# The head of an attention and feed-forward kernel: maxima on VectorE, half of the q sums on TensorE, and a new order of the instructions

## The chip, the cores and the metric

The kernel runs on one core of a Trainium2 chip. The metric is the time of one execution on the device in microseconds; of several runs the median is given. A profile is one such execution, recorded instruction by instruction.

## The reference, cut to what matters

```python
# q, k, v: 8 batches, 8 heads, 576 rows, 64 columns
q_s = exp(q - max over the 64 columns);  q_s /= sum over the 64 columns + 1e-9
k_s = exp(k - max over the 576 rows);    k_s /= sum over the 576 rows + 1e-9
kv  = einsum('bhsd,bhse->bhde', k_s, v)
x   = einsum('bhsd,bhde->bhse', q_s, kv)      # as 4608 tokens x 512
h   = x @ w_in                                # 512 -> 2048
out = (max(h, 0) + log1p(exp(-abs(h)))) @ w_out   # 2048 -> 512
```

Any shift that is the same over a normalised axis gives the same softmax up to the 1e-9, which the kernel uses below. The two weights come as 64-bit floats.

## The kernel before, in words

The 4608 tokens are cut into nine tiles of 512. The first three tiles go through the feed-forward part plainly; the other six go in pairs, as products of 2 x 2 blocks with seven instead of eight products. Each 512-column product of 32-bit numbers is made of three products of rounded high and low parts; only the first two of the sixteen weight blocks are used unsplit for tile 0.

Nothing schedules the kernel at run time: a long table `ORDER` names every step of the program in turn, and each engine executes its own steps strictly in that order, waiting by semaphores for the other engines. This document is about the head of the table, up to the first product with `w_out`. Its steps are:

- `b0 b1` fetch the q values of tile 0 in two halves, each as two transfers (`q_fetch`). `n` fetches keys and values of two heads at once (`kv_load`): 512 KB of main part on SyncE's DMA queue and a 64 KB tail on ScalarE's. The four pairs of heads of batch 0 are called pairs 0 to 3 here; in the order's rows the first two lie in tiles `kvt`, the others in `x_...`.
- `k0.h.i` is step i of pair h (`kv_unit`): 0 `top`, 1 `turn`, 2 `across`, 3 `spread`, 4 `shift`, 5 `power` (exp on ScalarE), 6 `product` (sums and k-times-v products on TensorE), 7 `scale` (a reciprocal on VectorE), 8 `keep` (two scaled copies on ScalarE). Before, `top` does nothing for batch 0; `turn` transposes the whole of k on TensorE into one PSUM bank, `across` takes the maximum along that bank on VectorE in three instructions (L500, L501, L504), `spread` sends it back to all partitions (L507), `shift` subtracts it (L511).
- `q0.i` are the steps of q's softmax on tile 0 (`q_unit`): a maximum by halves on VectorE (L580), four small copies on ScalarE that bring the neighbour's maximum (L567), their maximum (L591), subtraction (L594, one half on VectorE and one on GpSimd), exp (L597), sum by halves on VectorE (L600), one product with the matrix `pair` for each half (L607), which adds the sum of the other 32 rows, reciprocal (L625, L626), multiplication (L629).
- `x0.h.i` (`x_first`) transposes the normalised q, multiplies it by the kept k-times-v and copies the result; `B` is the first `w_in` block on it (L712), `U1` the second, `A0` the first softplus (L733 on ScalarE), `O0` the first product with `w_out` (L762).
- `T`, `M`, `S`, `J`, `P`, `Q` turn the 64-bit weights into 32-bit high and low parts on ScalarE, VectorE and GpSimd.
- `w` is a number of products of the identity with itself (L1163), whose result nobody reads.

ScalarE works through weight conversion and attention in one row, so a step of the one can wait behind a step of the other. The functions that the change touches:

Of the kernel before, what the change touches and what calls it, by code (L numbers as in the profile page):

```python
# [19 lines left out]
P = 128  # L20
# [32 lines left out]
    w0.20 b0 b1 q0.0 n k0.0.1 n q0.1 n n q0.2 q0.3 q0.4.1 l0 q0.5 l1 k0.0.2 k0.1.1 l2 k0.1.2 k0.0.3 k0.2.1 k0.0.4  # L53
    k0.0.5 q0.6 k0.1.3 k0.2.2 w5.5 k0.2.3 k0.1.4 k0.2.4 k0.1.5 l3 q0.7 k0.3.1 k0.3.2 k0.0.6 k0.0.7 T0 M0.1 T1 k0.1.6
    q0.8 k0.3.3 q0.12 w1.6 q0.13 k0.2.5 k0.2.6 k0.3.4 k0.3.5 k0.3.6 n M1.1 k0.0.8 q0.9 q0.10 w2.3 k0.1.7 w3.2 k0.2.7
    k0.1.8 k0.2.8 x0.0.0 w4.2 T2 x0.1.0 x0.1.1 x0.0.2 k0.3.7 k0.3.8 q0.11.1 x0.2.0 x0.3.0 x0.1.2 l4 J0 x0.3.1 x0.2.2
    k1.0.0 B0 B1 M2.1 n J1 T3 M3 x0.3.2 k1.0.1 k1.0.2 J2 S3.1 T4 M4.1 B2 B3 l5.6.7.8.9 L1 k1.0.3 k1.0.4 U0 k1.1.0
    k1.0.5 J4 U1 A0 k1.0.6 x0.2.3 k1.0.7 x0.2.4 O0 J3 P2 Q2 x0.0.3 x0.0.4 x0.1.3 T5 x0.3.3 x0.1.4 k1.1.1 x0.3.4 k1.1.2
    P3 Q3 A1 M5 k1.0.8 U2 T8 k1.1.3 k1.1.4 U3 P4 A2 q1.0 S5.1 T9 Q4 A3 G2 M6.1 O1 J5 G3 U4 k1.1.5 P5 O2 T6 M8.1 Q5.1
    k1.1.6 M7.1 T7 k1.2.0 k1.2.1 J6 J8 P6 k1.1.7 k1.2.2 q1.1 U5 A4 Q6 A5 J7 O3 U6 G4 G5 P7 M10 Q7 k1.1.8 O4 M9 q1.2  # L60
    T12 k1.3.0 U7 S9 q1.3 P8 A6 Q8 J9 T11 T10 A7 G6 q1.4 k1.3.1 O5 D4 P9 k1.2.3 G7 S10 M14.1 k1.2.4 q1.6 k1.3.2 O6
    M11.1 Q9 k1.2.5 U8 J11 A8 J10 P10 Q10 T14 U9 q1.8 A9 G8 M12.1 k1.2.6 k1.3.3 O7 P11 M13.1 Q11 J12 k1.3.4 G9 T13 P12
    q1.5 J13 q1.7 U10 Q12 J14 O8 U11 k1.3.5 A10 O9 k1.3.6 k1.2.7 U12 P13 A11 T15 Q13 q1.9 G10 q1.11 q1.10 P14 O10
    x1.0.0 A12 G11 U13 Q14 M15.1 k1.2.8 J15 x1.2.0 k1.3.7 P15 k1.3.8 Q15.1 U14 x1.1.0 A13 G12 D3 x1.1.3 O11 x1.3.0 U15
    G13 x1.0.4 x1.1.4 O12 x1.1.5 A14 x1.0.5 P0 Q0.1 k2.0.0 D6 G14 x1.3.3 D5 x1.2.4 k2.1.0 O13 x1.2.5 x1.3.4 P1 L2
    x1.3.5 D0 A15 Q1.1 G15 O14 k2.0.1 U16 k2.0.2 A16 D15 O15 U17 U18 A17 G16 k2.1.1 q2.1 Y0.1 k2.1.2 O16 G17 Y1.0 Y0.0
    q2.0 U19 k2.0.3 O17 A18 k2.1.3 k2.0.4 D1 G18 k2.1.4 Y0.2 D2 k2.0.5 q2.2 q2.3 Y1.2 D12 k2.1.5 Y2.1 A19 q2.5 O18
    Y1.1 D9 k2.1.6 k2.0.6 G19 D10 k2.0.7 q2.4.1 U20 Y2.0 Y2.2 n O19 U21 Y1.3 Y2.3 A20 Y0.3 D13 k2.0.8 Y2.4 Y2.5 G20
    Y1.4 O20 k2.2.0 U22 Y3.0 k2.1.7 A21 k2.2.1 D7 G21 k2.2.2 q2.6 q2.8 Y0.4 Y0.5 Y2.6 n D8 U23 q2.7 A22 k2.1.8 k2.2.3
    k2.3.0 Y3.2 O21 U24 G22 k2.3.1 k2.2.4 A23 q2.9 Y0.6 k2.3.2 A24 O22 q2.10 k2.3.3 k2.2.5 L3 Y1.5 H1.7.0 q2.11 x2.0.0  # L70
    D11 D14 k2.3.4 Y3.1 Y2.7 H1.7.1 U25 k2.2.6 k2.3.5 Y4.0 k2.2.7 Y2.8 k2.3.6 Y4.1 Y3.3 A25 Y1.6 O23 H1.8.0 U26 Y0.7
    k2.3.7 n A26 U27 Y3.4 x2.1.0 Y3.5 x2.2.0 H1.9.0 H1.8.1 O24 A27 Y3.6 H1.9.1 q3.0 O25 Y3.7 k2.3.8 k2.2.8 Y4.2
    H1.10.0 k3.0.0 n R0.0 Y3.8 H1.11.0 U28 k3.1.0 H1.10.1 x2.1.3 A28 q3.1 Y5.0 Y4.3 q3.12 x2.1.4 O26 Y0.8 Y4.4 k3.0.4
    H1.12.0 U29 q3.2 x2.1.5 U30 q3.3 k3.1.4 Y4.5 x2.0.4 H1.11.1 O27 x2.0.5 H1.12.1 A29 Y1.7 A30 U31 x2.3.0 H1.13.0
    x2.3.3 H1.13.1 k3.0.5 k3.1.5 q3.5 O28 q3.4 Y6.0 x2.3.4 Y7.1 R0.1 Y7.0 O29 x2.2.4 x2.2.5 R0.2 R0.3 q3.7 x2.3.5
    H1.14.0 Y6.1 L4 y0.1 H1.14.1 q3.6 A31 y0.0 R2.0 k3.1.6 Y7.2 k3.0.6 k3.0.7 Y1.8 Y6.2 Y4.6 q3.8 O30 H1.15.0 H1.15.1
    U32 n O31 n q3.13 y0.2 y1.0 A32 Y7.3 F1.0 Y4.7 U33 Y6.3 Y7.4 F1.2 Y6.4 q3.9 H2.0.0 k3.2.0 F1.3 y0.3 k3.3.0 R0.4
    y1.1 k3.2.4 A33 H2.1.0 U34 H2.0.1 F1.1 O32 k3.1.7 k3.2.5 k3.1.8 q4.0 q3.10 H2.1.1 y0.4 Y6.5 k3.0.8 y0.5 O33 k3.3.4
    A34 y1.2 k3.3.5 y2.0 k3.2.6 H2.2.0 Y4.8 q3.11 k3.3.6 H2.2.1 k3.2.7 U35 U36 R0.5 R0.6 y0.6 q4.1 Y7.5 A35 x3.1.0 n
    y0.7 y2.1 y1.3 y1.4 k3.3.7 q4.12 A36 k3.2.8 x3.0.0 y2.2 y1.5 U37 y1.6 n q4.2 q4.4 O34 k3.3.8 A37 H2.3.0 x3.2.0  # L80
    H2.3.1 k4.0.0 H2.4.0 q4.6 y0.8 k4.1.0 q4.3 q4.5 x3.3.0 k4.0.4 x3.1.3 x3.0.6 y1.7 O35 H2.4.1 k4.0.5 U38 O36 x3.1.6
    R0.7 x3.3.3 X0.1.hB11 R0.8 k4.1.4 k4.1.5 Y7.6 U39 A38 q4.8 x3.2.6 H2.5.0 q4.7 x3.3.6 y1.8 y3.1 q4.13 H2.5.1 A39
    X0.0.hB11 k4.0.6 q4.9 R0.9 n Y6.6 Y5.2 k4.1.6 k4.0.7 q4.10 O37 H2.6.0 U40 Y7.7 q4.11 H2.7.0 n H2.6.1 x4.1.0 Y6.7
    A40 x4.0.0 U41 k4.2.0 H2.7.1 R0.10 y4.0 X0.0.lB11 O38 y3.0 y2.3 Y7.8 R0.11 O39 y3.2 Y5.1 H2.8.0 k4.2.4 A41 k4.0.8
    y4.1 U42 Y5.3 k4.3.0 k4.1.7 R0.12 H2.8.1 O40 x4.2.0 k4.2.5 k4.3.4 U43 Y5.4 k4.3.5 y2.4 H2.9.0 k4.1.8 y4.2 A42 y4.3
    H2.10.0 A43 X0.1.lB11 y2.5 Y5.5 H2.9.1 y3.3 y4.4 k4.3.6 Y6.8 k4.2.6 H2.10.1 O41 R0.13 Y5.6 k4.2.7 k4.3.7 y5.0
# [124 lines left out]
def tile_attn_ffn(  # L211
# [1004 lines left out]
```

## Time and profile before

| | |
|---|---|
| median of 3 runs | 810.38 us (808.61 to 810.49) |
| the profiled execution | 809.8 us |
| its span, first instruction to last | 808.0 us |
| TensorE busy | 795.7 us (98%) |
| VectorE, ScalarE, GpSimd busy | 581.9, 499.7, 119.6 us |

The profiled execution lies 1.8 us above its span and 0.6 us under the median. TensorE's ends are modelled, so its busy time counts from one instruction's start to its modelled end; where instructions follow each other without a gap it reads as 100%.

### The profile page before, as it was taken

To read this page: it belongs to the slowest core of one execution; us is meant where nothing else is said; L and a number is where in the kernel's file an instruction comes from. 1 tells how busy PE (TensorE), PEld (TensorE's weight loads), DVE (VectorE), ACT (ScalarE), POOL (GpSimd) and SP (SyncE) were. 2 spreads that over 40 slices of the span, in tenths; PEclk is the share of its full clock that TensorE was granted. 3 is DMA by queue.
4 is the path that set the end of the run, shared out by engine and by line. 5 is a ranking of instruction groups with operands and counts; after the bars stand their busy time and mean duration, and the time that the engine had idled before them with its cause. 6 is when DMAs were issued, how large, how long until landed. Compare 5 with 4: busy or idle time off the path is not lost.

```text
span 808.0 us, 12020 instructions
## 1 busy us (share of the span) xinstructions
PE 795.7 (98%) x4312; PEld 637.7 (79%) x4312; DVE 581.9 (72%) x934; ACT 499.7 (62%) x826; POOL 119.6 (15%) x211
## 2 busy tenths in 40 slices
PE   7999999999999999999999999999999999999997
PEld 6668877887787878878788778887777888888886
DVE  6979764877799878549689898477688943136884
ACT  2999964674577557557768574658466633336651
POOL 1320021101011210001010004240000220400026
PEclk9999999999999999999999999999999999999999
DMA  9996176869788898889789448994483865858655
GB/s 302 360 323 239 30 238 260 307 207 343 256 279 279 290 334 294 292 244 294 233 247 303 151 166 251 299 283 158 141 259 124 262 196 178 266 175 287 193 159 88
DMA packets 118235, 193.73 MB, mean 240 GB/s; under 512 B 8416, under 2 KB 90592, under 8 KB 108960
## 3 DMA queue, kind: packets, MB, share of 16 engines
q1 hardware_dynamic: 114912, 186.67, 70.0%
q0 software_dynamic: 2944, 6.04, 3.6%
q8 instruction: 34, 0.56, 0.3%
q10 hardware_dynamic: 320, 0.26, 0.1%
q14 instruction: 25, 0.20, 0.1%
HBM read 149.95 MB, written 42.99 MB: 239 GB/s over the span
## 4 chain that ended last, share of the span: by engine, by line
PE 94%; DMA 2%; ACT 1%; issue 1%; DVE 1%; POOL 0%; SPq 0%; DVEq 0%
PE po L965 7%; PE po L967 6%; PE po L966 6%; PE po L851 6%; PE po L853 6%; PE po L852 6%; PE po L766 5%; PE ph L724 5%; PE ph L725 5%; PE ph L726 5%; PE po L768 5%; PE po L767 5%; PE ph L851 3%; PE ph L853 3%; PE ph L852 3%; PE ph L965 3%
## 5 line engine op out<-in xcount | busy, mean ns | idle before, releaser
L1010 POOL DMA_DIRECT2D out<-w x92 | 59.4, 653 | 232.0 <-DVE w L1002 230.5
L766 PE MATMUL po<-w,g_hi 128*128 128x512 f32 x164 | 65.6, 400 | 0.0
L724 PE MATMUL ph<-x,w 128*128 128x512 f32 x164 | 65.3, 398 | 0.0
L945 ACT CAST g_hi<-w 128x512 fp32r<-128x512 f32 x74 | 45.8, 621 | 29.8 <-PE po L966 17.2
L768 PE MATMUL po<-w,g_lo 128*128 128x512 f32 x164 | 64.0, 390 | 0.0
L767 PE MATMUL po<-w,g_hi 128*128 128x512 f32 x164 | 64.0, 390 | 0.0
L726 PE MATMUL ph<-x,w 128*128 128x512 f32 x164 | 63.9, 390 | 0.0
L725 PE MATMUL ph<-x,w 128*128 128x512 f32 x164 | 63.9, 390 | 0.0
L948 DVE TENSOR_TENSOR g_lo<-w,g_hi 128x512 fp32r<-128x512 f32 x74 | 50.1, 684 | 11.4 <-ACT g_hi L945 11.1
L742 DVE TENSOR_TENSOR g_lo<-g,g_hi 128x512 fp32r<-128x512 f32 x46 | 32.7, 712 | 32.1 <-ACT g_hi L739 32.1
L733 ACT ACTIVATE g<-ph 128x512 f32<-128x512 f32 x48 | 28.6, 599 | 39.3 <-PE ph L726 39.1
L932 DVE TENSOR_TENSOR w<-w,w 128x512 f32<-128x512 f32 x72 | 47.5, 683 | 5.6 <-ACT w L885 5.6
L479 POOL PARTITION_ALL_REDUCE mx<-mx x20 | 23.0, 1150 | 189.6 <-DVE mx L476 186.4
L874 DVE TENSOR_TENSOR w<-po,w 128x512 f32<-128x512 f32 x24 | 16.3, 684 | 45.6 <-PE po L853 24.7
L945 ACT CAST w<-w 128x512 fp32r<-128x512 f32 x52 | 31.8, 619 | 22.5 <-PE po L966 14.8
L851 PE MATMUL po<-w,x 128*128 128x512 f32 x112 | 44.2, 394 | 0.3 <-DMA x<-sums 0.3
L852 PE MATMUL po<-w,x 128*128 128x512 f32 x112 | 43.6, 389 | 0.0
L853 PE MATMUL po<-w,x 128*128 128x512 f32 x112 | 43.6, 389 | 0.0
L948 DVE TENSOR_TENSOR w<-w,w 128x512 fp32r<-128x512 f32 x52 | 35.3, 684 | 10.9 <-ACT w L945 10.7
L739 ACT CAST g_hi<-g 128x512 fp32r<-128x512 f32 x46 | 28.3, 620 | 21.2 <-PE po L767 14.0
L476 DVE TENSOR_REDUCE mx<-kvt 128x128 f32<-128x640 f32 x28 | 36.7, 1312 | 5.6 <-DMA kvt<-in_kv_tail 4.4
L766 PEld LDWEIGHTS po<-w,g_hi 128*128 128x128 f32 x164 | 30.8, 188 | 10.2 <-issue 1.7
(380 smaller groups left out, 2253.2 us busy)
## 6 DMA issues: line engine op xcount, KB each, us to landing
x<-sums SPq DMA_DIRECT2D x24, 1024.0 KB, 5.6
kvt<-in_kv SPq DMA_DIRECT2D x30, 512.0 KB, 6.8
kept<-w SPq DMA_DIRECT2D x15, 1024.0 KB, 8.8
w<-kept SPq DMA_DIRECT2D x13, 1024.0 KB, 7.1
x<-sums_out SPq DMA_DIRECT2D x44, 256.0 KB, 4.3
w<-kept SPq DMA_DIRECT2D x36, 256.0 KB, 5.4
x<-kept SPq DMA_DIRECT2D x36, 256.0 KB, 4.8
w<-sums_out SPq DMA_DIRECT2D x36, 256.0 KB, 5.3
```

What stands on the lines that cost most here:

```text
L724: nc.tensor.matmul(ph, lhsT=w_hi, rhs=x_hi, start=h == 0, stop=False)
L725: nc.tensor.matmul(ph, lhsT=w_lo, rhs=x_hi, start=False, stop=False)
L726: nc.tensor.matmul(ph, lhsT=w_hi, rhs=x_lo, start=False, stop=h == HP - 1)
L766: nc.tensor.matmul(po, lhsT=g_hi[:, ms], rhs=w_hi, start=j == 0, stop=False)
L767: nc.tensor.matmul(po, lhsT=g_hi[:, ms], rhs=w_lo, start=False, stop=False)
L768: nc.tensor.matmul(po, lhsT=g_lo[:, ms], rhs=w_hi, start=False, stop=j == NJ - 1)
L851: nc.tensor.matmul(ph, lhsT=w_hi, rhs=x_hi, start=c == 0 and i in (0, 4), stop=False, **more)
L852: nc.tensor.matmul(ph, lhsT=w_lo, rhs=x_hi, start=False, stop=False, **more)
L853: nc.tensor.matmul(ph, lhsT=w_hi, rhs=x_lo, start=False, stop=c == 1, **more)
L945: nc.scalar.copy(ring[p, i, s][0], right_of(p, i, s))
L948: engine.tensor_tensor(out=lo, in0=right_of(p, i, s), in1=hi.bitcast(F32), op=ALU.subtract)
L965: nc.tensor.matmul(bank, lhsT=w_hi, rhs=hi, start=begin, stop=False, **more)
```

## The change

- `top` now does work for batch 0: three maxima on VectorE reduce the five chunks of k to one (256, 128 and 128 columns wide). `turn` is then one transpose (L494) instead of ten, and `across` one reduction over 128 columns (L498).
- Tile 0's q gets a function of its own, `q_first`. The neighbour's maximum comes by one product for each half with a new matrix `other_half` (made by one subtraction on VectorE). The sum of a half can be taken on VectorE as before (`total`, L661) or on TensorE, as 32 accumulating products of `pair` with every 32nd column (L664); the new order takes the first half on TensorE and the second on VectorE. Each half has its own reciprocal.
- The two reciprocals of neighbouring pairs are taken by one instruction each (`scale`).
- The eight fills of the padding go from VectorE to GpSimd; GpSimd's first instruction that needs its library (`g`) comes behind them. One of q's two transfers of each half goes onto ScalarE's DMA queue, so q's four transfers stand two on each queue.
- There are fewer idle products of the identity (25 where there were 38), and they stand at other places.
- The rest of `ORDER` is new from end to end. The steps after the head are the same ones but stand in a changed sequence.

```diff
     def top():
+            mx = state["mx"] = sm.tile([P, 2, D], F32, name="mx", bufs=3)
             if not b:
+                two = sm.tile([P, 2, 2, D], F32, name="two")
+                for o, i0, i1 in (
+                    (two, kt[:, 0:2], kt[:, 2:4]), (mx, two[:, 0], two[:, 1]), (mx[0:TAIL], mx[0:TAIL], kt[0:TAIL, NCH]),
+                ):
+                    nc.vector.tensor_tensor(out=o, in0=i0, in1=i1, op=ALU.max)
                 return
...
         def turn():
-            if not b:
-                for c in range(NCH, -1, -1):
-                    rows = P if c < NCH else TAIL
-                    for z in range(2):
...
             nc.tensor.transpose(wide, state["mx"].rearrange("p z d -> p (z d)"), ident)
...
-                nc.sync.dma_start(out=qtiles[t][z * D:(z + 1) * D, 2 * g:2 * g + 2], in_=src[z, g])
+                queue = nc.sync if t or not z else nc.scalar
+                queue.dma_start(out=qtiles[t][z * D:(z + 1) * D, 2 * g:2 * g + 2], in_=src[z, g])
...
+    def q_first():
...
+        def cross(g):
+            nc.tensor.matmul(sums[:, (2 + g) * n:(3 + g) * n], lhsT=other_half, rhs=m[:, g], start=True, stop=True)
...
+        def total(g, on_pe=None):
+            if on_pe is None:
+                nc.vector.tensor_reduce(out=s[:, g], in_=half[g], op=ALU.add, axis=AX.X)
+                return
+            for e in range(32):
+                nc.tensor.matmul(
+                    sums[:, g * n:(g + 1) * n], lhsT=pair, rhs=half[g][:, :, e], start=e == 0, stop=e == 31
+                )
...
-    w0.20 b0 b1 q0.0 n k0.0.1 n q0.1 n n q0.2 q0.3 q0.4.1 l0 q0.5 l1 k0.0.2 k0.1.1 l2 k0.1.2 k0.0.3 k0.2.1 k0.0.4
...
+    w0.9 b0 b1 n n n n g q0.0 l0 q0.2 q0.1 w1.5 w2.2 q0.4 q0.3 w3.5 k0.0.0 q0.5 q0.6 q0.8 k0.0.1 k0.1.0 k0.0.2 w4.4
```

On TensorE's queue the head before had this, from the transposes of pair 2 (`x_178`) to the last spread (`m_266`, pair 3):

```order
L490 MATMUL po_126<-ident,x_178 64x128 x8
L507 MATMUL po_125<-ident,m_220 128x128
L1163 MATMUL ph_128<-ident 128x128 x5
L507 MATMUL po_126<-ident,m_239 128x128
L490 MATMUL ph_128<-ident,x_183 64x64 x2
L490 MATMUL po_127<-ident,x_183 64x128 x8
L522 MATMUL att_93<-one,kvt 64x1 x10
L527 MATMUL po_124<-kvt 64x64 x10
L522 MATMUL att_94<-one,kvt 64x1 x10
L527 MATMUL po_125<-kvt 64x64 x10
L507 MATMUL po_127<-ident,m_266 128x128
```

and the changed kernel has this in that place (`x_154` is pair 2, `x_159` pair 3, `po_128` the bank of pair 3):

```order
L494 MATMUL po_126<-ident,mx 128x128
L501 MATMUL po_125<-ident,m_201 128x128
L494 MATMUL po_127<-ident,mx 128x128
L501 MATMUL po_126<-ident,m_218 128x128
L664 MATMUL ph_130<-qt,pair 128x32 x32
L494 MATMUL po_128<-ident,mx 128x128
L669 MATMUL ph_130<-s,pair 128x32
L501 MATMUL po_127<-ident,m_235 128x128
L501 MATMUL po_128<-ident,m_275 128x128
L516 MATMUL att_93<-one,kvt 64x1 x10
```

The 32 products of the first q half (L664) now stand ahead of the transpose of pair 3's maxima (`po_128<-ident,mx`) and of the spreads of pairs 2 and 3, where the ten transposes of pair 3 stood free of them.

On VectorE's queue the same stretch was, from the shift of pair 2 to the multiplication of q's first half:

```order
L511 TENSOR_TENSOR x_178<-x_178,po_126 128x10x64
L600 TENSOR_REDUCE s<-qt 128x32
L500 TENSOR_REDUCE m_266<-ph_128 128x1
L501 TENSOR_TENSOR po_127<-po_127,m_266 128x1
L504 TENSOR_REDUCE m_266<-po_127 128x1
L535 TENSOR_SCALAR r<-att_93 128x1
L536 RECIPROCAL r<-r 128x1
L600 TENSOR_REDUCE s<-qt 128x32
L511 TENSOR_TENSOR x_183<-x_183,po_127 128x10x64
L625 TENSOR_SCALAR s<-ph_129 128x64
L626 RECIPROCAL s<-s 128x64
L629 TENSOR_TENSOR qt<-qt,s 128x1024
```

and is now, from pair 2's `across` on:

```order
L498 TENSOR_REDUCE m_235<-po_127 128x1
L505 TENSOR_TENSOR kvt<-kvt,po_126 128x10x64
L661 TENSOR_REDUCE s<-qt 128x32
L498 TENSOR_REDUCE m_275<-po_128 128x1
L672 TENSOR_SCALAR s<-ph_130 128x32
L675 RECIPROCAL s<-s 128x32
L672 TENSOR_SCALAR s<-ph_130 128x32
L675 RECIPROCAL s<-s 128x32
L505 TENSOR_TENSOR x_159<-x_159,po_128 128x10x64
L505 TENSOR_TENSOR x_154<-x_154,po_127 128x10x64
L531 TENSOR_SCALAR r_330<-att_93 128x2
L534 RECIPROCAL r_330<-r_330 128x2
```

One of the two long sums (L600, now L661) is gone; pair 3's `across` (`m_275`) is followed by both reciprocals, and the shifts of pairs 3 and 2 have moved behind them.

## Rows read from the trace of the kernel before

**Rows 1.** The page's first part: busy us, share of the span, instructions.

```profile
PE 795.7 (98%) x4312; PEld 637.7 (79%) x4312; DVE 581.9 (72%) x934; ACT 499.7 (62%) x826; POOL 119.6 (15%) x211
```

**Rows 2.** TensorE by stretch: length, busy us (records), granted clock, DMA share, GB/s.

```profile
3.00:5.00 2.00, 2.00 (x9) 1.00 1.03 277
12.00:14.00 2.00, 0.18 (x4) 1.00 1.02 408
14.00:16.00 2.00, 2.00 (x21) 0.53 1.03 412
100.00:700.00 600.00, 597.70 (x3200) 1.00 0.76 247
```

**Rows 3.** Timeline of TensorE at 40 us: start, length, line, operands, count.

```profile
40.93 3.42 PE L762 MATMUL po<-w,g 128*128 128x512 f32 x7
```

**Rows 4.** Timeline of ScalarE from 20 to 41 us; in brackets the idle time before.

```profile
23.68 0.73 ACT L517 ACTIVATE x<-x 128x640 f32<-128x640 f32 x1
25.03 0.74 ACT L517 ACTIVATE x<-x 128x640 f32<-128x640 f32 x1 [0.62 <-DVE x L511]
...
27.76 1.28 ACT L542 ACTIVATE kvs<-po,r 64x64 f32<-64x64 f32 x4 [0.42 <-DVE r L535]
...
30.61 0.58 ACT L691 COPY x<-po 128x512 f32<-128x512 f32 x1 [0.36 <-PE po L650]
...
40.27 0.60 ACT L733 ACTIVATE g<-ph 128x512 f32<-128x512 f32 x1
```

**Rows 5.** Timeline of VectorE from 5 to 13 us.

```profile
6.39 1.22 DVE L580 TENSOR_REDUCE m<-qt 128x32 f32<-128x1024 f32 x1 [2.86 <-DMA qt<-in_q]
...
9.86 1.22 DVE L580 TENSOR_REDUCE m<-qt 128x32 f32<-128x1024 f32 x1 [1.59 <-DMA qt<-in_q]
...
12.14 0.22 DVE L591 TENSOR_TENSOR m<-m,other 128x64 f32<-128x64 f32 x1 [0.40 <-ACT other L567]
12.40 1.22 DVE L594 TENSOR_TENSOR qt<-qt,m 128x1024 f32<-128x1024 f32 x1
```

**Rows 6.** Timeline of SyncE's DMA issues up to 17 us.

```profile
0.75 2.81 SPq L560 DMA_DIRECT2D qt<-in_q  x4
3.60 1.07 SPq L454 DMA_DIRECT2D kvt<-in_kv  x2
```

**Rows 7.** Timeline of all engines up to 42 us: TensorE and its weight loads.

```profile
2.98 6.77 PE L1163 MATMUL ph<-ident 128*128 128x128 f32 x40 [2.98 <-DVE ident L260]
...
10.86 1.09 PE L490 MATMUL po<-ident,kvt 128*64 128x128 f32 x16 [0.84 <-DMA kvt<-in_kv]
...
20.83 0.70 PE L522 MATMUL att<-one,kvt 128*64 128x1 f32 x20
...
24.87 0.30 PEld L607 LDWEIGHTS ph<-s,pair 128*128 128x128 f32 x2
24.98 0.31 PE L607 MATMUL ph<-s,pair 128*128 128x32 f32 x2
```

**Rows 8.** The same timeline: VectorE.

```profile
16.89 0.81 DVE L511 TENSOR_TENSOR kvt<-kvt,po 128x640 f32<-128x640 f32 x1
...
20.55 1.21 DVE L600 TENSOR_REDUCE s<-qt 128x32 f32<-128x1024 f32 x1
...
25.32 0.23 DVE L625 TENSOR_SCALAR s<-ph 128x64 f32<-128x64 f32 x1 [0.33 <-PE ph L607]
...
25.58 0.55 DVE L626 RECIPROCAL s<-s 128x64 f32<-128x64 f32 x1
```

**Rows 9.** Timelines of 33 to 37 us: VectorE.

```profile
35.03 0.29 DVE L504 TENSOR_REDUCE m<-att 128x1 f32<-128x128 f32 x1 [0.42 <-PE att L495]
```

**Rows 10.** Timeline of GpSimd up to 24 us.

```profile
9.49 0.18 POOL L1065 TENSOR_TENSOR first<-first 128x1 f32<-128x1 f32 x1 [8.65 <-issue]
12.45 2.95 POOL L594 TENSOR_TENSOR qt<-qt,m 128x1024 f32<-128x1024 f32 x1 [2.77 <-DMA kvt<-in_kv]
22.37 0.20 POOL L450 MEMSET kvt<- 64x128 f32 x1 [6.97 <-issue]
```

More of the change, by code (lines that the diff above doesn't have):

```diff
@@ L58 @@
[L58 to L62, printed above, removed]
@@ L241, in tile_attn_ffn @@
     pair = const.tile([P, P], F32, name="pair")
+    other_half = const.tile([P, P], F32, name="other_half")
     one = const.tile([P, 1], F32, name="one")
@@ L267, in make_tables @@
             )
+        nc.vector.tensor_tensor(out=other_half, in0=pair, in1=ident, op=ALU.subtract)
         nc.vector.memset(one, 1.0)
@@ L604, in swap @@
         def swap(g):
-            if not t:
-                nc.tensor.matmul(sums[:, 0:2 * n][:, g], lhsT=pair, rhs=s[:, g], start=True, stop=True)
-                return
             if not other:
@@ L633, in q_unit, with spread, top, join @@
             lambda: total(0), lambda: total(1), invert, lambda *e: divide(0, *e), lambda *e: divide(1, *e),
-        ] + ([cross, swap_all] if t else [lambda g=g: swap(slice(g * n, (g + 1) * n)) for g in range(2)])
+            cross, swap_all,
+        ]
+    def q_first():
+        n = TOK // 16
+        half = [qtiles[0][:, 2 * g:2 * g + 2].rearrange("p h (i r) -> p (h i) r", r=32) for g in range(2)]
+        m, s = (sm.tile([P, 2, n], F32, name=name) for name in ("m", "s"))
+        def spread(a, g):
+            return a[:, g].unsqueeze(2).broadcast_to([P, n, 32])
+        def top(g):
+            nc.vector.tensor_reduce(out=m[:, g], in_=half[g], op=ALU.max, axis=AX.X)
+        def cross(g):
+            nc.tensor.matmul(sums[:, (2 + g) * n:(3 + g) * n], lhsT=other_half, rhs=m[:, g], start=True, stop=True)
+        def join(g):
+            nc.vector.tensor_tensor(out=m[:, g], in0=m[:, g], in1=sums[:, (2 + g) * n:(3 + g) * n], op=ALU.max)
+        def shift(g, engine=nc.vector):
+            engine.tensor_tensor(out=half[g], in0=half[g], in1=spread(m, g), op=ALU.subtract)
+        def power(g):
+            nc.scalar.activation(half[g], half[g], AF.Exp)
+        def total(g, on_pe=None):
+            if on_pe is None:
+                nc.vector.tensor_reduce(out=s[:, g], in_=half[g], op=ALU.add, axis=AX.X)
+                return
+            for e in range(32):
+                nc.tensor.matmul(
+                    sums[:, g * n:(g + 1) * n], lhsT=pair, rhs=half[g][:, :, e], start=e == 0, stop=e == 31
+                )
+        def swap(g):
+            nc.tensor.matmul(sums[:, g * n:(g + 1) * n], lhsT=pair, rhs=s[:, g], start=True, stop=True)
+        def invert(g):
+            nc.vector.tensor_scalar(
+                out=s[:, g], in0=sums[:, g * n:(g + 1) * n], scalar1=EPS, scalar2=None, op0=ALU.add
+            )
+            nc.vector.reciprocal(s[:, g], s[:, g])
+        def divide(g, engine=nc.vector):
+            engine.tensor_tensor(out=half[g], in0=half[g], in1=spread(s, g), op=ALU.mult)
+        return [
+            lambda *e, g=g, f=f: f(g, *e)
+            for f in (top, cross, join, shift, power, total, swap, invert, divide) for g in range(2)
+        ]
     def x_part(t, h):
@@ L1165, in do @@
                 q_fetch(0, at)
+            elif kind == "g":
+                nc.gpsimd.tensor_tensor(out=first, in0=first, in1=first, op=ALU.add)
             elif kind == "n":
-                place = dict(engine=nc.vector, queue=nc.scalar) if ahead[0] < HP else {}
+                place = dict(queue=nc.scalar) if ahead[0] < HP else {}
                 if 2 <= ahead[0] < HP:
```

329 lines of the change are left out of this document (163 added, 166 removed).

## The prediction

> **What bounds the kernel now.** I read the page's first part, then TensorE by stretches, then the timelines of the first 41 us engine by engine. The profile's page says that TensorE is busy for 795.7 us, 98% of the span [rows 1]. The stretches say where it is not: from 100 to 700 us it lacks 2.3 us in 600 [rows 2], so behind the head the kernel is a dense row of products whose number the change leaves alone. What can move the time by much is therefore the moment at which this row begins, and whether the new order tears holes into it. I take as its beginning the first product with `w_out`, at 40.93 us [rows 3]; it waits for the first softplus, which ScalarE starts at 40.27 us [rows 4].
>
> ScalarE is the engine to follow backwards from there. Its timeline is almost closed from the third pair's exp at 23.68 us to the softplus at 40.27 us; the idle times in it are 0.62, 0.42 and 0.36 us [rows 4]. So between these two points lie 16.59 us, of which 15.2 us are work: two exps, eight kept copies, three copies of x, seven conversions of weights, the exp of the next batch's pair and a table load. By the code the new order has the very same instructions between its third k exp and its softplus, in another sequence. Hence one question decides: when does the third k exp start? If it starts 1.4 us later than now, at 25.1 us, and ScalarE then never waits, the softplus stands where it stood.
>
> Ahead of it VectorE is the engine to follow. Its first maximum waits until 6.39 us and its second until 9.86 us for q; the small copies on ScalarE cost it 0.40 us more, and it begins to subtract at 12.40 us [rows 5].
>
> **When pair 0 is there.** The new VectorE order needs the keys of pair 0 before it can join and subtract q's second maximum. Today TensorE takes them up at 10.86 us [rows 7]. SyncE issues q's four transfers in 2.81 us and the keys from 3.60 us on [rows 6]; with two of the four on ScalarE's queue the keys are issued 1.4 us earlier. If the issue sets the landing they land at 9.5 us. But the transfer engines are already full from 3 to 5 us (share 1.03, [rows 2]), and the same q bytes plus the tails still stand ahead. Then they land at 10.8 us. I take 10.2, between the two, since neither end has a row that excludes it. The Trainium skill, page DMA: Bandwidth & Descriptors, section Issuing engines are not separate DMA queues, says that transfers issued from several engines run on the same DMA engines and interleave. By that rule the split gains nothing here, the keys land at 10.8 us, and the sum below would be 810.2 us instead of 809.6; by the issue times alone it would be 808.9.
>
> **VectorE from pair 0 to pair 1's spread.** A full half of 1024 columns takes 1.22 us [rows 5], 640 columns 0.81 us [rows 8]; the slope gives about 0.40 us for 256 and 0.27 us for 128 columns, so a new `top` costs 1.0 us with its two inner waits. The transpose ends on VectorE in a reduction of 0.29 us [rows 9]. The row is: top 1.0, join 0.2 (as L591, [rows 5]), subtraction 1.2, top 1.0, across 0.3, top 1.0, across 0.3: 5.0 us, plus 0.1 for TensorE's spread. TensorE comes to the 32 products at 10.2 + 5.1 = 15.3 us. What the edits of this stretch remove (the fills, the copies on ScalarE, the long transposes) is already in this: q is subtracted at 12.4 us, as before, because a `top` of pair 0 stands ahead, and later VectorE has one long sum of 1.21 us [rows 8] less.
>
> **The 32 products.** They are the term that decides, and no row shows such a run. Each is a full 32-bit product, so it leaves two records with a load of 128 weight columns each, as the two records of L607 show: 64 loads. Bounds: the one-column products L522 run 20 records in 0.70 us, 0.035 us each, with half as many weight columns [rows 7]; that gives 64 x 0.035 = 2.2 us. At the other end, between 3 and 5 us nine records of the idle products take 2 us, 0.22 each [rows 2]; that gives 14.2 us. The nearest row has the same matrix and the same 32 columns: the load of L607 starts at 24.87 us and its product at 24.98 us, 0.11 us later, and the second load ends 0.30 us after the first began [rows 7]. I take 0.11 us for each load: 64 x 0.11 = 7.0 us. The products end at 22.3 us.
>
> The Trainium skill's page TensorE: Matmul & The Clock Gate, section LDWEIGHTS, makes a load cost its columns over 1.2 GHz; for 128 columns an estimate of 0.107 us, 6.8 us for the run, as the row has it. The Trainium skill lists on the same page, section Back-to-back issue gap, about 60 cycles for up to 64 moving columns; by that the run would take an estimated 1.6 us, and the time would be that of the first rival.
>
> **From there to the third exp.** Pair 3's transposed maxima stand behind the products on TensorE. Behind them come: the transpose 0.3, the reduction 0.3, two reciprocals with their additions 1.1 (for 64 columns 0.23 and 0.55 us, [rows 8]; for 32 I take 0.19 and 0.36 from the same fixed part), the subtraction 0.8 [rows 8], and a hand-over of 0.1: 2.6 us. The third exp starts at 22.3 + 2.6 = 24.9 us, the softplus at 24.9 + 15.2 = 40.1 us, 0.2 us before today's.
>
> VectorE meanwhile has, after pair 1's across at 15.2 us, only 4.1 us of work that does not need pair 3's transpose (a shift, the last top, an across, a shift, one sum): it stands idle from 19.3 to about 22.6 us. That is where the gain of the rebuilt head goes: 3.3 us of waiting for TensorE.
>
> **What costs nothing, and its cover.** GpSimd's first library instruction ends its wait at 9.49 us today [rows 10]. With eight fills of 0.20 us ahead [rows 10] it ends near 11.1 us; GpSimd's subtraction is asked for at 11.4 us, so it is hidden, and without that cover it would cost 0.3 us. Its exp stands behind pair 0's exp on ScalarE anyway. ScalarE issues two more transfers before its first exp, in time in which it waits for q. The extra subtraction for `other_half` lies in VectorE's wait for q, 2.86 us long [rows 5]. SyncE now fetches the next tile's q ahead of weight blocks 5 to 9; they are needed only after the first `w_out` product. At the very end of the kernel the last steps of each engine stand in the same sequence as before.
>
> **The sum.** 809.8 - 0.2 = 809.6 us against the profiled execution; the median of the runs shown is 0.6 us above that, so I predict 810.0 us.
>
> **The rivals.**
> 1. The products are cheap (2.2 us, the lower bound). They end at 17.5 us, VectorE is not held up, and the third exp follows its own row: 19.3 + 0.3 + 1.1 + 0.8 + 0.1 = 21.6 us, 3.5 us better than 25.1: 806.3 us. For it speaks that 32 columns are little work; against it the gap of 0.11 us at L607.
> 2. TensorE runs the products at half clock. Between 12 and 14 us it is busy for 0.18 us, and from 14 to 16 us the granted clock is 0.53, the lower level of 1.2 GHz for nearly all of it [rows 2]. The head after has 13 idle products fewer, and the new 32 stand just behind such a thin stretch. At 0.22 us a record they end 7.1 us later: 816.9 us, slower. It decides from 2.6 us of extra time on, that is if more than 24 of the 64 records run so. Against it: the 40 records of the idle products at the start take 6.77 us, 0.17 each [rows 7], so a continuous run gets faster on the way. Half of the run at that rate would be 813. The Trainium skill, page TensorE: Matmul & The Clock Gate, Part 1, says the same of an idle array: it falls back to half clock, and activity releases it. How it takes a long run of weight loads no run here shows.
> 3. The new order tears a hole into the dense part. Today's holes are 2.3 us in 600 [rows 2]; a second set and a little more is 2.5 us or over: about 813 us.
> 4. q's two halves really arrive side by side and pair 0 lands before 8 us: 807.6 us or less.
>
> **How the numbers follow.** My forecast, no measurable change, gets 0.55 with a range of its own of 808 to 812 (keys at 9.5 to 10.8 us, a partial clock fall, small holes). Rival 1 gets 0.17, rival 4 0.05, rival 2 in its slow form 0.10, rival 3 0.13. Under 0.3% (2.4 us) a measurement of this kernel tells little from no change. So faster 0.22, same 0.55, slower 0.23. The range reaches to rival 1 below and to rival 3 above and leaves out rival 2's full form and the far end of rival 4: 806.0 to 813.5 us.
>
> **What would show it.** In the profile after: the 32 products as one run of 64 records from about 15 us; its length (7 us, or 2, or 14) tells the first three cases apart. VectorE idle before pair 3's across by about 3 us; the third k exp near 25 us; the softplus near 40 us; TensorE between 100 and 700 us busy for about 597.7 us again. I am wrong if ScalarE waits for something else on its way (kept copies for their reciprocals, x for TensorE), if weight block 0 lands so late that its conversion pushes the exps, or if the dense part has changed.

## The result, and the profile after

The changed kernel takes 821.65 us (median of 4 runs, 819.55 to 822.0), the kernel before beside it 809.5 us (4 runs, 808.4 to 810.49). The ratio is 1.0142, with a 95% interval of 1.0123 to 1.0161: slower by 12 us. The profiled execution took 821.59 us, its span is 819.8 us. The forecast was 810.0 us, with a range of 806.0 to 813.5 us.

The page's first part says that TensorE is busier than before by 9.9 us, with 36 records fewer (columns as in [rows 1]):

```profile
PE 805.6 (98%) x4276; PEld 647.2 (79%) x4276; DVE 586.3 (72%) x929; ACT 509.5 (62%) x830; POOL 121.9 (15%) x219
```

So fewer records take more time. TensorE by stretches (columns as in [rows 2]) says where:

```profile
12.00:14.00 2.00, 0.30 (x3) 1.00 1.01 401
14.00:16.00 2.00, 0.52 (x2) 1.00 1.04 416
16.00:18.00 2.00, 1.92 (x12) 0.71 1.02 406
18.00:22.00 4.00, 4.00 (x21) 0.50 1.04 412
...
34.00:38.00 4.00, 4.00 (x80) 0.50 0.84 205
...
42.00:44.00 2.00, 2.00 (x9) 0.50 1.17 240
44.00:53.00 9.00, 8.39 (x40) 0.99 1.05 302
100.00:700.00 600.00, 598.57 (x3203) 1.00 0.75 244
```

One stretch of the changed kernel, and under it two of the kernel before, in the same columns:

```profile
16.80:44.10 27.30, 27.30 (x244) 0.50 0.62 202
```

```profile
14.13:17.54 3.41, 3.41 (x31) 0.50 1.04 416
17.60:41.00 23.40, 23.20 (x290) 1.00 1.02 366
```

In the changed kernel the granted clock is 0.50, that is 1.2 GHz, from 16.8 to 44.1 us without a break, although TensorE is busy throughout. Before, it was at half for 3.41 us only. The dense part from 100 to 700 us is as it was (598.57 us busy, 597.70 in [rows 2]).

TensorE's timeline (start, length, line, operands, count) shows the run of the 32 products, the x products and the first product with `w_out`:

```profile
16.44 13.37 PE L664 MATMUL ph<-qt,pair 128*128 128x32 f32 x64
...
39.59 3.69 PE L699 MATMUL po<-w,kvs 64*64 64x512 f32 x16
...
52.63 1.62 PE L811 MATMUL po<-w,g 128*128 128x512 f32 x3
```

The last row answers to [rows 3]: the dense row of products begins at 52.63 us instead of 40.93, 11.7 us later. From there to the end of the span it is 767.17 us, before 767.07 us. So the whole loss lies in the head, as the forecast said that it would.

ScalarE's timeline, from the exps of the third and fourth pair to the first softplus (brackets: the idle time before, and what ended it), answers to [rows 4]:

```profile
32.10 1.46 ACT L511 ACTIVATE x<-x 128x640 f32<-128x640 f32 x2 [9.74 <-DVE x L505]
...
34.73 1.34 ACT L545 ACTIVATE kvs<-po,r 64x64 f32<-64x64 f32 x4 [0.16 <-DVE r L534]
...
39.00 1.35 ACT L545 ACTIVATE kvs<-po,r 64x64 f32<-64x64 f32 x4 [1.74 <-DVE r L534]
41.64 1.07 ACT L740 COPY x<-po 128x512 f32<-128x512 f32 x2 [1.29 <-PE po L699]
...
48.11 0.74 ACT L511 ACTIVATE kvt<-kvt 128x640 f32<-128x640 f32 x1 [0.64 <-DMA qt<-in_q]
...
51.25 0.60 ACT L782 ACTIVATE g<-ph 128x512 f32<-128x512 f32 x1
```

The third exp waits 9.74 us, and starts at 32.10 us where 24.9 was forecast. Behind it ScalarE waits for 3.83 us more (0.16, 1.74, 1.29, 0.64), each time for something that TensorE made late, but for the last, which the profile puts down to a transfer.

VectorE's timeline, and under it GpSimd's, show what ended the one long wait and another stall ahead of it:

```profile
11.97 0.43 DVE L483 TENSOR_TENSOR two<-kvt 128x256 f32<-128x256 f32 x1
12.43 2.10 DVE L483 TENSOR_TENSOR mx<-two 128x128 f32<-128x128 f32 x1
...
30.11 0.29 DVE L498 TENSOR_REDUCE m<-po 128x1 f32<-128x128 f32 x1 [10.12 <-PE po L494]
```

```profile
12.48 1.90 POOL L654 TENSOR_TENSOR qt<-qt,m 128x1024 f32<-128x1024 f32 x1
```

VectorE stood for 10.12 us until the transpose of pair 3's maxima, queued behind the run, was done. And a maximum of 128 columns took 2.10 us while GpSimd subtracted; the same one takes 0.29 us for the other pairs.

The instructions of the run by line (durations in ns, least, median, most; first and last start) have two sorts of loads:

```profile
L664 PEld LDWEIGHTS ph<-qt,pair x64: 187/333/338, 16.3 to 29.3; 128*128 128x128 f32 x64
L664 PE MATMUL ph<-qt,pair x64: 217/401/402, 16.4 to 29.4; 128*128 128x32 f32 x64
```

The first few loads take 187 ns, most take 333. They overlap: 64 of them in 13.37 us are 0.209 us each, where the sum of the forecast had 0.11.

### The profile page after: what moved, and what is told of

It reads as the page before. It is cut to its first block, busy times and chain, and to the rows that moved or that the text cites. A ratio compares the mean times of both kernels' runs of the same rounds, so it can differ in the third digit from the quotient of the medians.

```text
span 819.8 us, 11986 instructions
## 1 busy us (share of the span) xinstructions
PE 805.6 (98%) x4276; PEld 647.2 (79%) x4276; DVE 586.3 (72%) x929; ACT 509.5 (62%) x830; POOL 121.9 (15%) x219
## 4 chain that ended last, share of the span: by engine, by line
PE 95%; DMA 2%; DVE 1%; SPq 1%; ACT 0%; issue 0%; ACTq 0%
PE po L1014 7%; PE po L1015 7%; PE po L1016 7%; PE po L900 6%; PE po L902 6%; PE po L901 6%; PE ph L773 5%; PE po L815 5%; PE ph L774 5%; PE po L816 5%; PE ph L775 5%; PE po L817 5%; PE ph L900 3%; PE ph L901 3%; PE ph L902 3%; PE ph L1014 3%
## 5 line engine op out<-in xcount | busy, mean ns | idle before, releaser
L791 DVE TENSOR_TENSOR g_lo<-g,g_hi 128x512 fp32r<-128x512 f32 x46 | 37.1, 811 | 31.4 <-ACT g_hi L788 31.3
L488 POOL PARTITION_ALL_REDUCE mx<-mx x20 | 26.7, 1337 | 169.5 <-DVE mx L485 155.6
L927 DVE TENSOR_TENSOR w<-po,g 128x512 f32<-128x512 f32 x24 | 16.5, 689 | 40.9 <-PE po L902 39.8
L485 DVE TENSOR_REDUCE mx<-kvt 128x128 f32<-128x640 f32 x28 | 37.0, 1320 | 2.8 <-DMA kvt<-in_kv_tail 2.6
```

## The experiments

The main theory: the granted clock decides. The run of 32 products is as cheap as forecast at full clock, but here it neither brought nor held full clock, and with TensorE at half clock the narrow products behind it are late as well. Its rivals: the run is dear by itself or holds up the wrong things behind it on TensorE; or the rebuilt head is slower by its own waits. The times in microseconds below are medians, and the last two columns are read from the one profiled execution of each kernel; the kernel before was measured on the same chip in each group, at 810.36, 810.34 and 809.55 us (e1 to e4, e5 to e8, e9 and e10).

| kernel | us (lowest to highest) | ratio to before, 95% interval | third k exp, us | first `w_out` product, us |
|---|---|---|---|---|
| changed | 821.65 (819.55 to 822.0) | 1.0142 (1.0123 to 1.0161) | 32.10 | 52.63 |
| e1 sum on vector | 813.41 (812.42 to 814.0) | 1.0037 (1.0026 to 1.0048) | 23.70 | 43.67 |
| e2 clock kept | 817.34 (816.23 to 820.78) | 1.0095 (1.0065 to 1.0125) | 27.97 | 48.30 |
| e3 products in old head | 827.1 (820.53 to 827.55) | 1.0179 (1.0138 to 1.022) | 22.40 | 56.74 |
| e4 old head, few idle | 817.43 (815.94 to 820.8) | 1.0085 (1.0055 to 1.0114) | 23.20 | 43.69 |
| e5 clock filled | 810.0 (809.22 to 812.0) | 1.0004 (0.9991 to 1.0017) | 23.63 | 41.45 |
| e6 subtract on vector | 810.02 (809.37 to 811.46) | 0.9996 (0.9984 to 1.0008) | 23.52 | 41.36 |
| e7 idle within run | 815.72 (815.26 to 818.96) | 1.0074 (1.0052 to 1.0096) | 32.33 | 49.70 |
| e8 pair 3 ahead | 823.79 (821.85 to 827.04) | 1.017 (1.0143 to 1.0196) | 23.00 | 55.45 |
| e9 fewer idle | 808.59 (807.05 to 812.03) | 0.9984 (0.9967 to 1.0002) | 23.02 | 39.74 |
| e10 exps first | 809.93 (808.92 to 816.0) | 1.0005 (0.9985 to 1.0026) | 22.50 | 42.50 |

**e1, the first half's sum on VectorE.** The changed kernel without the run (pieces of `ORDER`):

```diff
-T0 q0.10.1
-k0.3.1 q0.11 q0.13 k0.3.2
+T0 q0.10
+k0.3.1 q0.11 q0.13 q0.12 k0.3.2
```

> The changed kernel with the sum of q's first half back on VectorE and one product with the pair matrix, as the second half has it; the 32 products are gone. Products theory (the run of 32 products is the loss: 13.4 us on TensorE, all else follows from it): the third k exp starts near 23.5 us instead of 32.1, and the time is 807 to 810 us. Clock theory (the new head keeps TensorE so thinly busy that its granted clock falls to half at 16.8 us and stays there until the 512-column products, whatever the run does): the clock still falls near 17 us, the k products still take 2.06 us a pair instead of 1.15, and the time stays at 812 to 816 us.

813.41 us, in the 812 to 816 of the clock theory and 3.05 us over the kernel before: of the 12.15 us that the changed kernel loses, 9.1 go with the run. The third exp stands where it did before (23.70, before 23.68 us), but the softplus comes 2 us late, and TensorE by stretches says why:

```profile
14.00:34.60 20.60, 15.58 (x187) 0.50 0.91 318
34.60:44.00 9.40, 8.79 (x44) 1.00 1.04 309
```

Even without the run TensorE stays at half clock, through all the k products and the x products, to 34.6 us. Here the k products take 2.1 us for a pair (before 1.2) and the x products 3.68 us. A second cost, then, that the forecast's sum did not have.

**e2, idle products that keep the clock up to the run.** 15 more idle products ahead of the run, which stays:

```diff
-k0.0.2 w4.4
+k0.0.2 w4.16
-k0.1.1 k0.0.3 k0.2.0
+k0.1.1 k0.0.3 w3.3 k0.2.0
```

> The changed kernel with 15 more products of the identity, 12 behind the first transposed maxima and 3 behind the first spread, so that TensorE has work from 11 to 16 us, where it was idle for 3.3 us ahead of the 32 products. Clock theory: the granted clock is full when the run begins, the run takes about 7.2 us (64 loads of 0.11) instead of 13.4, and what follows goes at full clock: 810 to 813 us. If the run itself lets the clock fall, it falls inside it: 815 to 819 us. Products theory in its strict form (a record costs 0.21 us at any clock): the run stays at 13.4 us, 819 us or more.

817.34 us, in the 815 to 819 that were expected if the clock falls inside the run. The run now takes 8.66 us. TensorE's stretches, with the run's own instructions alone (busy time of products and of loads, granted clock, DMA share, GB/s), show both prices in one run:

```profile
17.00:22.00 5.00, 4.99 (x46) 5.00 (x46) 1.00 1.03 407
22.60:25.60 3.00, 3.00 (x15) 2.94 (x14) 0.50 0.59 236
```

At full clock 46 records take 5.00 us, 0.109 us each: the 0.11 of the forecast. Then the clock falls in the middle of the run, with TensorE never idle, and a record takes 0.2 us. The k and x products behind it stay at half clock.

**e3, the same run in the old head.** The kernel before, with q's first half summed by the 32 products instead of on VectorE:

```diff
-q0.7 k0.3.1
+k0.3.1
+                if g.start == 0:
+                    for e in range(32):
+                        nc.tensor.matmul(
+                            sums[:, 0:n], lhsT=pair, rhs=half[0][:, :, e], start=e == 0, stop=e == 31
+                        )
+                    return
```

> The kernel before with one part of the change alone: the sum of q's first half as 32 accumulating products in place of VectorE's sum and its one product, at the place of that product (23.3 us in the trace of before, clock full there and seven idle products behind). Products at full clock cost 0.11 us a load: the run takes 7.2 us, the products of pairs 2 and 3 come some 6 us later, and the time is 814 to 816 us. If the run lets the clock fall: records go from 0.11 to 0.21 us inside it, and 817 to 821 us. If the products are cheap at full clock (0.035 us a record): 2.2 us, and 808 to 811 us.

827.1 us, the slowest of all, and 6 us over the highest range expected. TensorE by stretches, the run in its timeline, and the wait that decides in ScalarE's:

```profile
22.00:24.00 2.00, 2.00 (x35) 1.00 1.04 390
24.00:26.00 2.00, 2.00 (x16) 0.77 1.13 271
26.00:30.00 4.00, 4.00 (x21) 0.50 1.02 332
```

```profile
22.76 11.59 PE L609 MATMUL ph<-qt,pair 128*128 128x32 f32 x64
```

```profile
41.13 1.29 ACT L542 ACTIVATE kvs<-po,r 64x64 f32<-64x64 f32 x4 [15.04 <-DVE r L535]
```

The old head brings TensorE to the run at full clock, and there too it falls, and stays at 0.50 to 44 us. The run stands behind the spreads here and does not delay the third exp (22.40 us); instead ScalarE waits 15.04 us for a reciprocal that comes only behind the run. So neither the rebuilt head nor the new order is needed for a loss of this size.

**e4, the old head with few idle products.** The kernel before, with 11 idle products at the start less and those between the steps left out:

```diff
-w0.20 b0
+w0.9 b0
-q0.12 w1.6 q0.13
+q0.12 q0.13
```

(`w5.5`, `w2.3`, `w3.2` and `w4.2` go as well.)

> The kernel before with 9 instead of 20 idle products at the start and none of the 18 later ones; nothing else. Clock theory: TensorE's granted clock falls earlier or stays down longer than the 3.4 us of before (14.1 to 17.5 us), the k and x products of the head run at half speed, and the time is 811 to 815 us. Products theory: nothing of weight changes, 809 to 810 us.

817.43 us, over the expected 811 to 815. In the profiled execution the clock falls twice; the second time catches the x products and the first blocks of `w_in`:

```profile
26.00:30.00 4.00, 2.72 (x33) 0.69 1.03 340
30.00:34.00 4.00, 4.00 (x12) 0.50 1.08 360
34.00:38.00 4.00, 4.00 (x6) 0.53 1.03 410
```

The x products take 5.75 us there. The first `w_out` product is 2.8 us late; from it to the end of the span it is 771.0 us instead of 767.1, by new gaps in the dense part whose cause was not followed. So leaving out the idle products, whose results nobody reads, cost time; e4 leaves out 29 of them, the change 13. How much of it is the clock stays open: two of e4's four executions list a mean granted clock of 0.999 and 1.000 and took 820.8 and 815.94 us all the same, and no trace of them is kept.

**e5, e1 with TensorE's gaps filled.** e1, and idle products where TensorE waits or runs narrow products:

```diff
-k0.0.2 w4.4
+k0.0.2 w4.16
-k0.1.1 k0.0.3 k0.2.0
+k0.1.1 k0.0.3 w3.3 k0.2.0
-k0.1.3 k0.0.5
+k0.1.3 w5.4 k0.0.5
-k0.3.1 q0.11 q0.13
+k0.3.1 w6.9 q0.11 w7.4 q0.13
```

(and three behind each pair's `k0.h.6`).

> Both q sums on VectorE as in e1_sum_on_vector, and 44 idle products of the identity more, laid into the places where TensorE waits or runs narrow products (12 before the maxima of pair 1, 3 and 4 before the transposes of pairs 2 and 3, 13 before the q sums, 3 behind each pair's k products). Theory (what e1_sum_on_vector loses is the half clock from 14 to 34.6 us): the granted clock stays at 1.00, the k products of a pair take 1.15 us, the x products about 1.9 us; third k exp near 23.2 us, first softplus near 39.5 us, first product with w_out at 39.5 to 41 us, 808.5 to 810.5 us. Rival (the rebuilt head is slower by its own waits, not by the clock; idle products only stand in the way): as e1_sum_on_vector or later, first w_out product at 43.7 us or more, 813 us or over.

810.0 us, within the expected 808.5 to 810.5. The granted clock is 1.00 in every stretch from 12 to 42 us; two of them, and the x products in the timeline:

```profile
18.00:20.00 2.00, 1.95 (x17) 1.00 1.06 418
...
26.00:28.00 2.00, 2.00 (x47) 1.00 1.05 279
```

```profile
30.77 1.95 PE L699 MATMUL po<-w,kvs 64*64 64x512 f32 x16
```

It is 3.4 us faster than e1, by products that compute nothing, and e1's 3.05 us over the kernel before are gone. With that the clock is shown as the cause of e1's loss. The first `w_out` product is at 41.45 us, half a microsecond after the expected range.

**e6, both halves of q subtracted on VectorE.** e5 with `q0.7.1` replaced:

```diff
-q0.7.1 l1 k0.1.1
+q0.7 l1 k0.1.1
```

> As e5_clock_filled, but both halves of q are subtracted on VectorE, none on GpSimd. Theory (VectorE's 128x128 maximum of pair 1 took 2.0 instead of 0.29 us because GpSimd's subtraction ran beside it): the maximum takes 0.29 us, VectorE has 1.2 us more of its own and 1.75 us less of standing, so the third k exp comes about 0.5 us earlier than in e5_clock_filled: 0.3 to 0.6 us less in the time. Rival (the maximum was late for another reason, as a wait for pair 1's values): it stays late and the whole is 1 us longer than e5_clock_filled.

VectorE's maximum of pair 1 no longer stands:

```profile
12.98 0.29 DVE L483 TENSOR_TENSOR mx<-two 128x128 f32<-128x128 f32 x1
```

The stall is explained. The gain expected of it did not come: the third exp is 0.11 us earlier than e5's where 0.5 was expected, and the time is not measurably another (810.02 us), since VectorE's own 1.21 us for the second half take most of the 1.5 to 1.8 us that the stall had cost (1.93 instead of 0.41 us in e5, 2.10 instead of 0.29 in the changed kernel).

**e7, idle products inside the run.** e2, and one idle product behind every second of the 32:

```diff
+                if e % 2:
+                    nc.tensor.matmul(warm[:, 0:P], lhsT=ident, rhs=ident, start=True, stop=True)
```

> As e2_clock_kept (16 instead of 4 idle products ahead of pair 1's transpose, 3 more ahead of pair 2's), and one idle product behind every second of the 32 products. Theory (the run of weight loads itself lets the clock fall, products of 128 columns among it keep it): granted clock 1.00 to the end of the run, the run takes 64 x 0.112 + 32 x 0.107 = 10.6 us instead of 8.7, third k exp near 30 us, but the k and x products behind it run at full clock for the most part: first w_out product at 46 to 48 us, 815 to 817 us. Rival (idle products don't keep it): the clock falls in the run as in e2_clock_kept, the run takes 13 us or more, 820 us or over.

815.72 us, inside the expected 815 to 817, though the run has 32 records more than in e2. TensorE by stretches and the run's instructions by line:

```profile
20.00:30.00 10.00, 10.00 (x92) 1.00 0.47 185
30.00:36.00 6.00, 5.90 (x169) 1.00 0.35 101
```

```profile
L664 PEld LDWEIGHTS ph<-qt,pair x64: 190/192/192, 19.3 to 29.7; 128*128 128x128 f32 x64
```

The clock holds through the run, every load takes the short 190 to 192 ns, and the whole of 96 records takes 10.7 us (19.38 to 30.09), as the expected 10.6. It holds for the k products behind it too, which no idle product accompanies. The third exp (32.33 us) and the first `w_out` product (49.70 us) come later than expected in this profile: it is of the slowest of the five executions (818.96 us), q's second half arrived late in it, the clock was at half from 11.9 to 15.3 us, ahead of the run, and the run began only at 19.38 us. ScalarE's timeline gives what the forecast had called its 15.2 us:

```profile
32.33 1.46 ACT L511 ACTIVATE x<-x 128x640 f32<-128x640 f32 x2 [7.28 <-DVE x L505]
...
47.41 0.60 ACT L784 ACTIVATE g<-ph 128x512 f32<-128x512 f32 x1
```

15.08 us at full clock. (The last 1.75 us ahead of the `w_out` product TensorE waits for the next tile's q.)

**e8, pair 3 ahead of the run.** The changed kernel with the transpose of pair 3 and the spreads of pairs 2 and 3 ahead of the 32 products:

```diff
-T0 q0.10.1
-k0.3.1 q0.11 q0.13 k0.3.2 q0.15 q0.14 k0.1.5 k0.2.3 M0.1 k0.3.3 k0.0.6 k0.3.4 T1
+T0
+k0.3.1 k0.3.2 k0.2.3 k0.3.3 q0.10.1 q0.11 q0.13 k0.3.4 k0.2.4 k0.1.5 q0.15 q0.14 M0.1 k0.0.6 T1
```

> As the changed kernel, but the transpose of pair 3's maxima and the spreads of pairs 2 and 3 stand ahead of the 32 products on TensorE, and the shifts of pairs 2 and 3 ahead of the reciprocals on VectorE. Theory (the run's own length holds TensorE, whatever stands behind it; only its first victim is the third exp): third k exp near 21 us instead of 32.1, but the k products of pair 0 start only when the run ends at 32 us, and the first w_out product comes at 48 to 51 us: 817 to 820 us. Rival (the order is the fault: the transposed maxima behind the run): ScalarE never waits again, first w_out product at 42 us or earlier, 811 us or less.

823.79 us, 4 us over the expected range. The run, from TensorE's timeline, and the wait that took the place of the old one, from ScalarE's:

```profile
20.13 13.70 PE L664 MATMUL ph<-qt,pair 128*128 128x32 f32 x64
```

```profile
38.06 1.34 ACT L545 ACTIVATE kvs<-po,r 64x64 f32<-64x64 f32 x4 [12.69 <-DVE r L534]
```

The third exp is at 23.00 us, and nothing is won by it: the k products stand behind the run instead, and the wait moves 15 us down ScalarE's row. That the order alone was the fault is refuted. The time was missed because the run began later than assumed, behind waits for pair 3's maxima, and because ScalarE still had 15.78 us from the first kept copies to the softplus (53.84 us).

**e9, without the idle products behind the k products.** e6 less `w8.3`, `w9.3`, `w10.3` and `w11.3`, since e7 had them unneeded.

> As e6_subtract_on_vector without the 12 idle products behind the k products. Theory (in e7_idle_within_run the k products held the full clock by themselves, 30 to 36 us at 1.00; the idle products behind them only delay the second reciprocals and the x products): the k products of a pair take 1.17 us and follow each other, granted clock 1.00 throughout, ScalarE's waits of 1.36 and 0.79 us shrink to about 0.5 in sum, softplus near 39.3 us, first product with w_out near 39.9 us: 808.2 to 809 us. Rival (the k products do not hold the clock here): it falls behind 24 us, the x products take 3.7 us, first w_out product at 41.5 us or later, 810 us or over.

808.59 us, 0.9984 (0.9967 to 1.0002) of the time before: the fastest median of all, but not told apart from no change. The granted clock is 1.00 in every stretch from 12 to 42 us, the k products follow each other at about 1.2 us a pair, and the dense row begins 1.2 us earlier than before, near the 39.9 us expected:

```profile
39.74 3.87 PE L811 MATMUL po<-w,g 128*128 128x512 f32 x8
```

**e10, the exps ahead of the sums.** e9 with the shifts of pairs 2 and 3 ahead of q's sums, and fewer idle products in that place:

```diff
-k0.3.1 w6.9 q0.11 w7.4 q0.13 q0.12 k0.3.2 q0.15 q0.14 k0.1.5 k0.2.3 M0.1 k0.3.3 k0.0.6 k0.3.4 T1 k0.3.5 q0.17.1 k0.1.6 k0.2.4
+k0.3.1 k0.3.2 k0.2.3 k0.3.3 k0.3.4 k0.2.4 k0.1.5 w6.3 k0.0.6 k0.1.6 q0.10 q0.11 q0.13 q0.12 q0.15 q0.14 M0.1 T1 k0.3.5 q0.17.1
```

> As e9_fewer_idle, with the spreads and shifts of pairs 2 and 3 ahead of both q sums on VectorE, and the k products of pairs 0 and 1 ahead of the q sums' products on TensorE; 3 idle products ahead of them instead of 13. Theory (with the sums on VectorE the third exp waits for them, 1.2 us, and the k products behind them on TensorE too): third exp at 22.2 us without a wait, x products near 28.7 us, softplus near 38.5 us, first w_out product near 39.2 us: 807.5 to 808.5 us. Rival (q then becomes the late one: the divided and transposed q comes no earlier, or the clock falls in the thinner stretch): x products no earlier than 30 us, 809.5 us or over.

809.93 us, the rival's time, by the second of its reasons. The third exp comes at 22.50 us without a wait, but the clock falls:

```profile
22.00:24.00 2.00, 2.00 (x28) 0.50 1.04 416
...
32.00:34.00 2.00, 2.00 (x9) 0.50 0.79 208
```

and the x products, which start at 29.00 us, take 4.18 us instead of e5's 1.95. So this order won 0.5 us at the third exp and lost more behind it, in part to the clock; a multiplication on VectorE was 1.36 us longer as well (last section). Its interval tells it apart neither from the kernel before nor from e9.

## Why the prediction was wrong

The step that failed is the price of the 32 products: "I take 0.11 us for each load". The row behind it [rows 7] was of a stretch at full clock, and the forecast kept that clock for the run and for all that follows. In the changed kernel the run went at half clock, at 0.209 us a record. At full clock the price was right, and the cheap products of the first rival are excluded: e2's 46 records took 0.109 us each.

The reason given against the rival of half clock, that "a continuous run gets faster on the way", rested on the idle products at the start, which have 128 columns behind each load; the 32 products have 32. A later stretch of the kernel before shows them again (columns as in [rows 2]):

```profile
7.00:9.00 2.00, 2.00 (x18) 1.00 1.05 253
```

A record takes 0.11 us here and 0.22 us from 3 to 5 us [rows 2]. The 1.00 of that earlier row is not a reading: the trace's records of the granted clock begin only at 7.30 us, and the time ahead of them counts as 1.00. So the run that the forecast saw getting faster may have begun at half clock, as its 0.22 us, near the 0.209 of the 32 products, suggest.

In the changed kernel, e2, e3 and e8 the run of loads with 32 columns behind each lost full clock or did not get it back; in e7, with idle products among them, it kept it. The Trainium skill, page TensorE: Matmul & The Clock Gate, Part 1, says that activity of the array releases the half clock. In the changed kernel the clock rose at 44.15 us, among products of 512 columns, which agrees; through the run, which keeps TensorE busy from 16.44 to 29.62 us, it stayed at 0.50 from 16.84 us on, and here the measurement decides. The Trainium skill's price of a load, on the same page in the section LDWEIGHTS, an estimated 0.107 us for 128 columns, agrees with e2's 0.109 us at full clock; at half clock the run's 0.209 us stand against it, and decide.

Step by step, for the profiled execution:

- *Keys of pair 0 at 10.2 us*: at least 0.6 us early. VectorE took up the first maximum of pair 0 at 9.62 us and its tail at 10.41 us without waiting for either, nearer to the forecast's end by the issue times (9.5) than to the other (10.8). (The forecast's "q is subtracted at 12.4 us" does not fit its own row, which gives 11.4; it was 10.71.)
- *TensorE at the 32 products at 15.3 us*: 16.44 us, 1.1 us late. The maximum of pair 1 that stood under GpSimd's subtraction cost 1.8 us; the earlier keys gave some back. The forecast had looked at GpSimd's subtraction only for when it is asked for, not for what it does to VectorE. e6 shows the cause. Nor was the wait for GpSimd's library hidden: the first instruction that needs it came at 12.32 us instead of "near 11.1", and GpSimd's subtraction only behind it, at 12.48, though VectorE had begun its own half at 10.71.
- *The run, 7.0 us*: 13.2 us (16.44 to 29.62), 6.2 us more. This is the term that was mis-sized.
- *2.6 us from the run to the third exp*: 2.5 us. Right.
- *15.2 us from the third exp to the softplus*: 19.15 us, 3.95 more; the waits of 0.16, 1.74 and 1.29 us are for k and x products at half clock, and 0.64 are the wait put down to a transfer. e7's 15.08 us show that the count was right for full clock.
- *Softplus to the first `w_out` product*: 1.38 us instead of the 0.66 before, 0.7 us more. TensorE waits 0.61 us for VectorE's maxima of the next batch's keys (L485), and not for the softplus, which ends at 51.85 us. Nor does the trace before show a wait for it: TensorE comes straight from 20 narrow products (L527, from 40.20 us), and the softplus ends at 40.87 us.
- *The dense part unchanged*: right, 767.17 us from there to the end.

The sum is 1.1 + 6.2 - 0.1 + 3.95 + 0.7 = 11.85 us on top of 809.6: 821.45 us, and the profiled execution took 821.59. That the gain would be eaten by VectorE waiting for TensorE was right too: 10.12 us of waiting where 3.3 were forecast. The forecast's "one question decides: when does the third k exp start?" did not hold: in e3 and e8 it starts at 22.40 and 23.00 us, ahead of the 23.68 before, and they are the two slowest kernels.

Of the rivals the second, half clock, is what happened. It said 816.9 us and fell short by 4.7 us, for the most part because it charged half clock to the 64 records alone and not to the 80 k products and 8 x products behind them; the late start of the run (1.1) and the end (0.7) come on top, and the run itself was 0.9 us cheaper than this rival had it. The part behind the run does not need the run: e1 has it alone, and e5 takes it away. That rival had a chance of 0.10; its own words ("the new 32 stand just behind such a thin stretch") and the row that showed 0.53 from 14 to 16 us [rows 2] were worth more.

## What to carry to other kernels

Ask of every new run of narrow products at which clock it will run, and price it at both: a price taken from a row at full clock holds only if something holds that clock. The stretch just ahead does not settle it: in the changed kernel it was thin, but in e2 and e3 it was at 1.00 and the clock fell inside the run. Idle products that look like waste can be a part of the schedule (e4, e5), and some are not (the 12 that e9 leaves out); before any of them goes, price the narrow products behind it at half clock. And where a step is moved out of the way of a long run, look for what else stands behind that run: in e8 the wait came back further down ScalarE's row, at the kept copies.

## What was not expected of the hardware

- A run of 64 loads with 32 columns behind each did not hold the granted clock: it fell from 1.00 to 0.50 in the middle of the run in e2 and e3, was at 0.50 over all but the first 0.4 us of it in the changed kernel, and over all of it in e8. With one 128-column product after every second of the 32 it stayed at 1.00 (e7). By what rule the chip grants the clock is left open; these cases are all that is shown.
- A maximum on VectorE with two operands in SBUF stood while GpSimd's subtraction ran: 2.10 us instead of 0.29 in the changed kernel, and with pair 2's values 1.93 us instead of 0.41 in e5. In e10 VectorE's multiplication of q's half met GpSimd's of the other half:

```profile
25.55 2.56 DVE L678 TENSOR_TENSOR qt<-qt,s 128x1024 f32<-128x1024 f32 x1
```

  It takes 1.20 us in e5. Before, it was GpSimd that stood: its subtraction started just after VectorE's own and took 2.95 us [rows 10], in the changed kernel 1.90. The Trainium skill, page SBUF — State Buffer, section SBUF: two separate sides, has this as an exclusive lock of a shared pair of ports, which whoever comes first holds for its whole instruction. The rows agree with the lock: the one that stands ends only after the other has ended. They do not show who comes first: VectorE's record starts 0.05 us ahead of GpSimd's both before (12.40 against 12.45 us, where GpSimd stood) and in the changed kernel (12.43 against 12.48, where VectorE stood). For this kernel it is a wash, by e6.
